# Layer two's pairs: the x tile and the last operand rounded at the end of the pair in front, and the next pair's transpositions ahead of the last output tile's addition

## The chip, the cores and the metric

The kernel runs on one core of a Trainium2 chip. A core has five engines that run their own queues of instructions side by side: TensorE (PE in the profile; its weight loads are listed apart as PEld), VectorE (DVE), ScalarE (ACT), GpSimd (POOL) and SyncE (SP), which here issues most of the DMAs. They wait for each other on semaphores. The metric is the time of one execution on the device in microseconds; with one core, the slowest core is the only one. All times below are microseconds.

## The reference

Four blocks act on one residual stream `x` of 2048 tokens by 512 features, in float32: linear attention, gMLP, and both once more with the same weights.

```python
# linear attention: 32 heads of 16
qkv = layernorm(x) @ wqkv                 # 512 x 1536
phi = lambda t: where(t > 0, t + 1, exp(t)) + 1e-6
kv  = einsum("bhsd,bhse->bhde", phi(k), v)
z   = einsum("bhsd->bhd", phi(k))
o   = einsum("bhqd,bhde->bhqe", phi(q), kv) / (phi(q) . z + 1e-6)
x   = x + o @ wo

# gMLP
t   = gelu(layernorm(x) @ w_in)           # 512 x 1792
z1, z2 = t[..., :896], layernorm(t[..., 896:])
g   = einsum("ts,bsf->btf", w_sp, z2) + b_sp
x   = x + (z1 * g) @ w_out
```

## The kernel before

The tokens are worked on in 16 tiles of 128. A *page* is a tile of 128 by 512 float32. TensorE multiplies in a rounded format, so every operand is kept as two parts: a *high* part, the value rounded (ACT, line 136, `high`), and a *low* part, the rounded rest (DVE, line 139, `low`). A product of two operands is then three matmuls (lines 150 to 152, `mm3`): high by high, high by low, low by high.

The change lies at the start of the second linear attention (`P1` with `L == 1`). Its input was normalised tile by tile while the first gMLP produced it, and went to DRAM (`norm`, line 394, on ACT; `send`). The first ten tiles are worked in five *pairs* `p` of tiles `a = 2p` and `b = 2p + 1`; the other six follow one by one in `second`. A pair does two things:

- The projections on K and Q. Two tiles together are brought through seven products (`P1`, `P7`, `P2`, `P6`, `P5`, `P4`, `P3`, in this order) in place of eight, six matmuls each, from sums of halves of the rows and sums of quarters of the weights (`joint`). The operands of a pair are `A` (tile a transposed), `B` (tile b, overwritten by a difference), `S` (a sum) and `D`, the *last operand*, half a page, that only `P3` reads.
- The accumulation of G, from which kv comes: `Gmm`, 24 matmuls of lines 150 to 152 in a pair, of the keys (phi of K) with the normalised tile itself, the *x tile*. These run one pair behind the projections: pair `p` makes the Gs of pair `p - 1`.

Around the products stand, by line:

- `rows` (448, DVE) turns a loaded tile by a transposition of 1.09; `first_part`, `second_part`, `sum_part` round A, B and S; `pair_sums` (841 to 846, DVE) makes the sums on half pages; `last_part` splits the half page D.
- ACT copies the accumulator of `P1` (bank `A`) into bank `B` (line 918), copies E to `w` (936) and B to `u` (949). DVE adds `X = w + B` (961 in pair 0, 977 in the others) and `c = E + u` (1008). `P2` and `P6` run behind the copy, `P3` behind X.
- phi: ACT does a relu and an exponential (871, 872, `pair_phi`), DVE the two halves of its sum (882, `pair_out`), four passes of ACT and four sets of halves a pair: A, X, c and B (`last`), the last two in the following pair. The keys are split into high (569, ACT) and low (905, DVE).
- The x tiles are loaded again from DRAM (`loadx`, 476, SP), and split by `x_high` (ACT) and `x_low` (DVE), lines 136 and 139.
- POOL adds up phi of K (`zsum`, 899). `wait_for` (892) is a tiny POOL operation that only orders a `zsum` behind a DVE operation.
- `own.staged()` are steps of background work for the last block, sums of quarters of `w_sp` (DMA in, DVE, POOL, DMA out). `side` holds pieces of the next weights `wo` and `win2`, whose rounding (136, 139, into `bg` tiles) stands in the last pair and in `second`.

The order on each engine is the order in which the program is written; nothing reorders it. Buffers are handed out by pools (`pages`, `banks`, `quads`): a DMA that loads a page waits until the reader of its last content is done. In pair 0 stands the end of the block in front too: `last_o`, which multiplies the last output tile of gMLP, adds it to the stream (2157, DVE), and computes its statistics (373, 375 on DVE, three small operations on POOL, the last at 384); then come `norm(15)` and `send(15)`.

```python
            if p:
                r = self.pair_phi(last)
                self.key_low(b - 2)
                self.x_high(b - 2)
                self.x_low(b - 2)
```

Of the kernel before, what the change touches and what calls it, by code (L numbers as in the profile page):

```python
# [15 lines left out]
P = 128  # L16
# [3 lines left out]
NT = S // P  # L20
# [7 lines left out]
PAIRS = (NT - DEFER) // 2  # L28
# [63 lines left out]
def mixer_kernel(ctx: ExitStack, tc: tile.TileContext, x_in, wqkv, wo_d, win1_d, win2_d, wsp_d, bsp_d, wout_d,  # L92
# [9 lines left out]
    pages = Slots(main, "pg", 23)  # L102
    quads = Slots(main, "qd", 6)
# [348 lines left out]
    class P1:  # L452
# [454 lines left out]
        def pair(self, p, side):  # L907
            a, b, own = 2 * p, 2 * p + 1, inner["N4"]
            nxt = p + 1 if p + 1 < PAIRS else None
            self.turn.load(a + 2)  # L910
            if nxt is not None:
                self.turn.load(b + 2)
            A = banks.get(PAGE)
# [5 lines left out]
            if p:  # L919
                c, last = self.open  # L920
                r = self.pair_phi(c)
                self.pair_out(c, r, b - 2, 0)
                self.K_high(b - 2)
            else:
                self.last_o()
                spare = quads.get([P, 2, 2, 512])
                own.home = Views(pages, spare)
                self.spare = spare
# [36 lines left out]
            if nxt is None:  # L965
                self.turn.row(a + 2)
            else:
                self.rows(a + 2)
                self.first_part(nxt)
                if p:  # L970
                    self.wait_for(self.ops[nxt, "A"][1][:, 0, 0:1])
            if p:
# [5 lines left out]
            r = self.pair_phi(X)  # L978
            if nxt is not None:
                self.rows(b + 2)  # L980
                self.pair_sums(nxt, 0)
                self.pair_sums(nxt, 1)
            else:
                self.T_high(a + 2)
# [8 lines left out]
            banks.put(X)  # L993
            if nxt is not None:
# [15 lines left out]
            self.product(B, "P3", p)  # L1010
            self.open = c, B
            if nxt is None:
                for _ in range(2):
                    side.popleft().piece()
            own.staged(False)
            if p >= PAIRS - 2:
                side[0].fetch()
                side[0].fetch()

        def second(self, side):  # L1020
            own = inner["N4"]
# [4 lines left out]
            for s in range(NT - DEFER + 1, NT + 2):  # L1026
                self.turn.load(s + 1)
                first = s == NT - DEFER + 1
                if first:
                    self.loadx(s - 1)  # L1030
                    self.loadx(s)
                self.loadx(s + 1)
                if first:
# [4 lines left out]
                    r = self.pair_phi(last)  # L1038
                    self.keys(s - 2)
# [723 lines left out]
    class P4:  # L1763
# [380 lines left out]
        def o(self, i, nxt):  # L2144
            q = self.zs.pop(i)
            b = banks.get(PAGE)
            for f in range(NF):
                mm3(b, (q[:, 0, f, :], q[:, 1, f, :]), self.wout[f], f == 0, f == NF - 1)
            quads.put(q)
            x = self.x.pop(i)  # L2150
            out = xs[2 * self.L + 2, i]
# [15 lines left out]
        def run(self, nxt):  # L2167
# [81 lines left out]
            for i in range(NT):  # L2249
# [6 lines left out]
                if nxt is not None and i == NT - 1:  # L2256
                    nxt.last_o = lambda: self.last(nxt)
                    break
                self.o(self.order[i], nxt)
                if nxt is not None:  # L2260
# [6 lines left out]
        def last(self, nxt):  # L2267
            i = NT - 1
            self.o(i, nxt)
            nxt.ms[i] = stats(nxt.x[i])  # L2270
            nxt.send(i - 1)
            self.join(i, nxt)

        def join(self, i, nxt):
# [34 lines left out]
            elif i > 11:  # L2309
                inner["N4"].staged()  # L2310
            if i == 15:
                for m in range(2):
                    for j in range(2):
                        w.parts(m, j, (4,))
                        w.done(m, j + 2)

# [46 lines left out]
```

## Time and profile before

| what | us |
|---|---|
| median of 3 runs (lowest to highest) | 1375.51 (1375.13 to 1376.03) |
| the profiled execution | 1374.01 |
| its span, first to last instruction | 1372.3 |
| PE busy in it | 1354.6 |
| DVE, ACT, POOL busy in it | 1061.7, 659.1, 504.6 |
| pair 0 and pair 1, from the first matmul of P1 on | 681.96, 697.17 |
| pairs 2, 3, 4 | 717.84, 735.62, 753.40 |
| behind the pairs; PE without a hole again | 771.10; 785.30 |

A row of a timeline has the start, the duration, the engine, the line, the operation, output and inputs (the program's names, buffer numbers left out), the shapes, and in brackets how long the engine sat idle before it and what ended that. A window is a stretch of time with the busy time and the number of instructions of each engine in it. The *granted clock* is the share of TensorE's full clock that it had in a stretch; 0.50 is half. PE's busy time counts a slow matmul at its slow length.

### The profile page before, as it was taken

The page shows a single profiled execution, that of the slowest core. Times are in us where ns is not written, and L with a number is a line of the kernel's source. Part 1 is how long each engine was busy: PE and PEld are TensorE (multiplying, and loading weights), DVE is VectorE, ACT ScalarE, POOL GpSimd, SP SyncE. Part 2 cuts the span into 40 slices and gives each one's busy share as a digit, 9 for nine tenths or more (in the row PEclk, how much of TensorE's full clock was granted, in tenths as well). Part 3 has the DMA queues.
Part 4 walks back from the last instruction along what each step waited for, and adds up shares of the span by engine and source line. Part 5 has one row for each costly group of instructions (what it writes and reads, how often), then busy time and mean ns, then how long its engine had stood idle before and what let it go on. Part 6 is the DMA issues. An engine that isn't in the chain of part 4 may idle for free.

```text
span 1372.3 us, 18447 instructions
## 1 busy us (share of the span) xinstructions
PE 1354.6 (99%) x6055; PEld 1126.8 (82%) x6055; DVE 1061.7 (77%) x1674; ACT 659.1 (48%) x1067; POOL 504.6 (37%) x603
## 2 busy tenths in 40 slices
PE   9999999999999999999989899999999999999998
PEld 7888888888888888888866688888888888888887
DVE  7885888876866888978977768877767798988642
ACT  7775543446443343424566665454456534534310
POOL 3333476533393347428411124633230011212240
PEclk9999999999999999999999999999999999999999
DMA  5762479966797988878652433766668798688552
GB/s 191 228 211 87 134 256 318 306 205 201 254 345 263 305 292 279 287 272 291 192 172 70 123 109 116 230 227 213 211 204 276 234 338 321 225 267 295 221 184 89
DMA packets 181744, 310.17 MB, mean 226 GB/s; under 512 B 15696, under 2 KB 67920, under 8 KB 177552
## 3 DMA queue, kind: packets, MB, share of 16 engines
q1 hardware_dynamic: 166544, 251.45, 56.2%
q0 software_dynamic: 11504, 51.12, 10.4%
q10 hardware_dynamic: 3600, 6.42, 1.3%
q8 instruction: 47, 0.77, 0.2%
q14 instruction: 49, 0.40, 0.1%
HBM read 211.68 MB, written 97.26 MB: 225 GB/s over the span
## 4 chain that ended last, share of the span: by engine, by line
PE 93%; DVE 4%; ACT 2%; issue 1%; DMA 0%; DVEq 0%; SPq 0%; ACTq 0%
PE bank L152 16%; PE bank L151 16%; PE bank L150 16%; PE bank L2019 9%; PE bank L2020 9%; PE bank L2021 9%; PE bank L1953 4%; PE bank L1952 4%; PE bank L1950 4%; PE bank L1389 1%; PE bank L1390 1%; PE bank L1388 1%; DVE pg L139 1%; DVE pg L448 1%; PE bank L404 1%
## 5 line engine op out<-in xcount | busy, mean ns | idle before, releaser
L2019 PE MATMUL bank<-qd,pg 128*128 128x512 f32 x544 | 211.7, 389 | 0.5 <-DVE bg L2078 0.5
L2021 PE MATMUL bank<-qd,pg 128*128 128x512 f32 x544 | 211.6, 389 | 0.0
L2020 PE MATMUL bank<-qd,pg 128*128 128x512 f32 x544 | 211.6, 389 | 0.0
L1866 DVE TENSOR_TENSOR qd<-qd,qd 128x1024 fp32r<-128x1024 f32 x104 | 139.4, 1341 | 63.0 <-ACT qd L1857 62.4
L1857 ACT ACTIVATE qd<-qd 128x1024 fp32r<-128x1024 f32 x104 | 110.1, 1058 | 121.2 <-DMA qd<-in_wsp_dram 42.6
L136 ACT ACTIVATE pg<-pg 128x512 fp32r<-128x512 f32 (+1 forms) x150 | 90.9, 613 | 115.0 <-DVE pg L448 37.2
L380 POOL TENSOR_SCALAR rs<-mv 128x1 f32<-128x1 f32 x96 | 44.7, 465 | 256.8 <-DVE mv L375 238.0
L2041 POOL TENSOR_TENSOR bg<-bg,pg 128x512 f32<-128x512 f32 x56 | 88.0, 1583 | 113.6 <-DMA pg<-z 100.9
L139 DVE TENSOR_TENSOR pg<-pg,pg 128x512 fp32r<-128x512 f32 (+1 forms) x147 | 108.4, 739 | 18.5 <-ACT pg L136 14.2
L2019 PEld LDWEIGHTS bank<-qd,pg 128*128 128x128 f32 x544 | 102.1, 188 | 22.1 <-issue 0.9
L2021 PEld LDWEIGHTS bank<-qd,pg 128*128 128x128 f32 x544 | 102.1, 188 | 21.2
L2020 PEld LDWEIGHTS bank<-qd,pg 128*128 128x128 f32 x544 | 102.1, 188 | 21.0
L152 PE MATMUL bank<-qd,pg 128*128 128x512 f32 x300 | 117.4, 391 | 0.0
L1609 POOL TENSOR_TENSOR pg<-pg,pg 128x512 f32<-128x512 f32 x50 | 78.5, 1570 | 104.8 <-DMA pg<-in_wsp_dram 80.0
L448 DVE STREAM_TRANSPOSE pg<-pg 128x512 f32<-128x512 f32 x79 | 86.3, 1092 | 10.5 <-DMA pg<-yt 6.2
L150 PE MATMUL bank<-bg,qd 128*128 128x448 f32 x256 | 94.0, 367 | 0.0
L151 PE MATMUL bank<-bg,qd 128*128 128x448 f32 x256 | 93.6, 366 | 0.0
L152 PE MATMUL bank<-bg,qd 128*128 128x448 f32 x256 | 93.4, 365 | 0.0
L1950 PE MATMUL bank<-qd,pg 128*128 128x512 f32 x224 | 87.1, 389 | 0.0
L1952 PE MATMUL bank<-qd,pg 128*128 128x512 f32 x224 | 87.1, 389 | 0.0
L1953 PE MATMUL bank<-qd,pg 128*128 128x512 f32 x224 | 87.1, 389 | 0.0
L150 PE MATMUL bank<-wo,qd 128*128 128x512 f32 x224 | 87.1, 389 | 0.0
(293 smaller groups left out, 3359.4 us busy)
## 6 DMA issues: line engine op xcount, KB each, us to landing
qd<-s SPq DMA_DIRECT2D x64, 512.0 KB, 4.5
qd<-n POOLq DMA_DIRECT2D x32, 1024.0 KB, 7.9
pg<-in_wsp_dram SPq DMA_DIRECT2D x99, 256.0 KB, 5.0
qd<-in_wsp_dram SPq DMA_DIRECT2D x40, 512.0 KB, 4.4
n<-pg SPq DMA_DIRECT2D x74, 256.0 KB, 4.7
pg<-z SPq DMA_DIRECT2D x56, 256.0 KB, 5.0
x<-pg SPq DMA_DIRECT2D x48, 256.0 KB, 2.7
pg<-x SPq DMA_DIRECT2D x48, 256.0 KB, 3.7
```

Of the source, the lines that this page charges most:

```text
L139: nc.vector.tensor_sub(l, src, h.bitcast(F32))
L150: nc.tensor.matmul(out, ah, bh, start=start, stop=False)
L151: nc.tensor.matmul(out, ah, bl, start=False, stop=False)
L152: nc.tensor.matmul(out, al, bh, start=False, stop=stop)
L1857: nc.scalar.activation(wh, r, AF.Copy)
L1866: nc.vector.tensor_sub(wl, r, wh.bitcast(F32))
L1950: m(out[i], h[:, o, f], w[:, o, 0], start=first and name in ("P1", "P2", "P5"), stop=False, skip_group_check=True)
L1952: m(out[i], h[:, o, f], w[:, o, 1], start=False, stop=False, skip_group_check=True)
L1953: m(out[i], l[:, o, f], w[:, o, 0], start=False, stop=last and name in ("P2", "P3", "P4"), skip_group_check=True)
L2019: m(out, h[:, o], w[:, 0, j, :], start=start, stop=False, skip_group_check=True)
L2020: m(out, h[:, o], w[:, 1, j, :], start=False, stop=False, skip_group_check=True)
L2021: m(out, l[:, o], w[:, 0, j, :], start=False, stop=stop, skip_group_check=True)
```

## The change

Seven moves, all in `pair`, `second` and what they call:

1. The x tile of `b` is split (`x_high`, `x_low`) at the end of the pair that loads it, behind `c`, and no longer in the following pair between phi and `w`.
2. The last operand of the next pair (`last_part`) is split there too; for pair 0 it keeps its place in pair 0, ahead of which `last_o` is gone.
3. In pair 0 the next pair's rows, first operand and half sums come ahead of the sum X. In pairs 1 to 3 only one of the two half sums (845, 846) moves, behind DVE's halves of X.
4. The last output tile's matmuls stay early (`o`); its addition, statistics, `norm(15)` and `send(15)` (`o_out`, `last`) come at the end of pair 0, behind the splits of points 1 and 2.
5. In the last pair, two of the four pieces of the next weight stand ahead of X, the other two ahead of `c`; their loads (`fetch`) move with them.
6. Behind the pairs, the x tile of the last `a` is split by `xsplit(s - 3)` ahead of G, and a `wait_for` and two `zsum` stand there.
7. Rows and x tiles are loaded at other places: those of pair 1 in front of pair 0, where `join` issues them during the block in front, and in `second` two of the three x tiles later. `join` no longer issues the quarter sums of the weights (`w.parts`), which pair 0 now does.

The core of the diff (line numbers behind it grow by up to 23):

```diff
@@ pair
             if p:
+                self.turn.load(a + 2)
...
                 self.K_high(b - 2)
-            else:
-                self.last_o()
...
-            self.last_part(p)
-            if p:
                 r = self.pair_phi(last)
                 self.key_low(b - 2)
-                self.x_high(b - 2)
-                self.x_low(b - 2)
+            else:
+                self.last_part(p)
+                w = self.joint
+                for m in range(2):
+                    for j in range(2):
+                        w.parts(m, j, (4,))
+                        w.done(m, j + 2)
+                o = self.before
+                o.ob = o.o(NT - 1, self)
+                self.send(NT - 2)
+                own.staged()
+                self.spare = quads.get([P, 2, 2, 512])
...
                 nc.scalar.activation(u, B, AF.Copy)
+                self.rows(a + 2)
+                self.first_part(nxt)
+                self.rows(b + 2)
+                self.pair_sums(nxt, 0)
+                self.pair_sums(nxt, 1)
                 self.product(A, "P2", p)
                 self.product(B, "P5", p)
                 X = banks.get(PAGE)
...
                 self.turn.row(a + 2)
-            else:
+                for _ in range(2):
+                    side.popleft().piece()
+                for _ in range(2):
+                    side[0].fetch()
+            elif p:
...
-            if p == 0:
-                self.norm(NT - 1)
-                self.send(NT - 1)
             self.loadx(b)
...
                 self.turn.load(b + 2)
-                for _ in range(2):
-                    side.popleft().piece()
-                side[0].fetch()
-                side[0].fetch()
+                side.popleft().piece()
+                side.popleft().piece()
...
             self.open = c, B
+            self.x_high(b)
+            if nxt is not None:
+                self.last_part(nxt)
+            self.x_low(b)
+            if p == 0:
+                self.last_o()
+                self.norm(NT - 1)
+                self.send(NT - 1)
+            own.staged(False)
@@ second
-                    self.xsplit(s - 2)
-                    self.keys(s - 3)
+                    self.K_high(s - 3)
+                    self.key_low(s - 3)
+                    self.xsplit(s - 3)
+                    self.wait_for(self.xhl[s - 3][1][:, 0:1])
+                    self.zsum(s - 2)
+                    self.zsum(s - 3)
                     self.Gmm(s - 5, (2, 3))
...
                     self.Gmm(s - 2)
-                    self.xsplit(s - 3)
+                    self.loadx(s)
+                    self.loadx(s + 1)
                     self.xsplit(s - 1)
```

**DVE, pair 0.** From the last output tile's addition (2157) to the sum X of pair 0 (961), before; the rows with `qd2` are quarter sums of the weights, `pg18_723` is the last operand's low part, 1750 a background step.

```order
L2157 TENSOR_TENSOR pg10_710_6858<-pg10_710_6858,bank3_182_6975 128x512
L373 BN_STATS st_6999<-pg10_710_6858 128x6
L375 BN_AGGR mv_7001<-st_6999 128x2
L139 TENSOR_TENSOR pg20_704_6803<-pg20_704_6803,pg19_717_6948 128x512
L1750 TENSOR_TENSOR pg2_718_6951<-pg2_718_6951,pg14_709_6856 128x512
L139 TENSOR_TENSOR qd2_159_7016<-pg15_665_6275,qd2_159_7016 128x256
L139 TENSOR_TENSOR qd2_159_7016<-pg6_677_6391,qd2_159_7016 128x256
L139 TENSOR_TENSOR qd2_159_7016<-pg16_666_6277,qd2_159_7016 128x4x2x32
L139 TENSOR_TENSOR qd2_159_7016<-pg9_678_6393,qd2_159_7016 128x4x2x32
L139 TENSOR_TENSOR pg18_723_7026<-pg5_698_6744,pg18_723_7026 128x256
L961 TENSOR_TENSOR bank1_183_7051<-w0_7029,bank7_181_6973 128x512
```

The same stretch of DVE now, from the first background step to X, which stands in line 973:

```order
L139 TENSOR_TENSOR pg20_704_6803<-pg20_704_6803,pg8_719_6952 128x512
L1770 TENSOR_TENSOR pg4_720_6955<-pg4_720_6955,pg14_709_6856 128x512
L448 STREAM_TRANSPOSE pg7_724_7028<-pg10_710_6858 128x4x128
L139 TENSOR_TENSOR pg5_725_7032<-pg7_724_7028,xA1_7030 128x512
L448 STREAM_TRANSPOSE pg15_726_7034<-pg0_716_6909 128x4x128
L841 TENSOR_TENSOR pg6_727_7036<-pg15_726_7034 128x256
L842 TENSOR_TENSOR pg15_726_7034<-pg7_724_7028,pg15_726_7034 128x256
L845 TENSOR_TENSOR pg6_727_7036<-pg6_727_7036,pg7_724_7028 128x256
L846 TENSOR_TENSOR pg7_724_7028<-pg7_724_7028,pg6_727_7036 128x256
L973 TENSOR_TENSOR bank1_183_7053<-w0_7018,bank7_181_6973 128x512
```

The two transpositions with their rounding and sums are ahead of X; the addition and the statistics of the last output tile are gone from here (five half pages stand in front of the first row shown).

**ACT, end of pair 0 and start of pair 1.** Before, with the normalisation (394) ahead of xB and xS, the operands B and S of pair 1, and then the copy (918):

```order
L394 ACTIVATE pg3_731_7080<-pg10_710_6858,nb_7006,rs_7003 128x4x4x32
L136 ACTIVATE xB1_7090<-pg9_729_7069 128x512
L136 ACTIVATE xS1_7094<-pg5_730_7071 128x512
L918 ACTIVATE bank4_186_7137<-bank2_184_7123 128x512
L871 ACTIVATE pg22_739_7139<-c0_7109 128x512
```

Now:

```order
L136 ACTIVATE xB1_7077<-pg15_726_7034 128x512
L136 ACTIVATE xS1_7081<-pg6_727_7036 128x512
L136 ACTIVATE pg2_738_7104<-pg3_733_7071 128x512
L136 ACTIVATE pg19_740_7107<-pg7_724_7028 128x256
L394 ACTIVATE pg15_741_7122<-pg1_711_6860,nb_7120,rs_7117 128x4x4x32
L922 ACTIVATE bank4_186_7146<-bank2_184_7132 128x512
L871 ACTIVATE pg6_744_7148<-c0_7096 128x512
```

The normalisation now stands directly ahead of the copy of pair 1, behind the x tile (`pg2_738`) and the last operand (`pg19_740`).

**ACT, pair 2.** From the rounding of S to `w` (936), before; `pg_767` is the last operand, `pg_769` the x tile.

```order
L136 ACTIVATE xS_7252<-pg_756_7231 128x512
L918 ACTIVATE bank_194_7290<-bank_192_7276 128x512
L871 ACTIVATE pg_764_7292<-c_7264 128x512
L872 ACTIVATE pg_764_7292<-pg_764_7292 128x512
L569 ACTIVATE pg_765_7297<-pg_758_7244 128x512
L136 ACTIVATE pg_767_7300<-pg_752_7209 128x256
L871 ACTIVATE pg_768_7303<-bank_186_7137 128x512
L872 ACTIVATE pg_768_7303<-pg_768_7303 128x512
L136 ACTIVATE pg_769_7307<-pg_757_7236 128x512
L936 ACTIVATE w_7311<-bank_193_7283 128x512
```

Now, with the copy in line 922 and `w` in 943:

```order
L136 ACTIVATE xS_7254<-pg_756_7231 128x512
L136 ACTIVATE pg_764_7274<-pg_759_7236 128x512
L136 ACTIVATE pg_766_7277<-pg_754_7211 128x256
L922 ACTIVATE bank_194_7299<-bank_192_7285 128x512
L871 ACTIVATE pg_769_7301<-c_7266 128x512
L872 ACTIVATE pg_769_7301<-pg_769_7301 128x512
L569 ACTIVATE pg_770_7306<-pg_760_7244 128x512
L871 ACTIVATE pg_772_7309<-bank_186_7146 128x512
L872 ACTIVATE pg_772_7309<-pg_772_7309 128x512
L943 ACTIVATE w_7313<-bank_193_7292 128x512
```

Both roundings moved from behind the copy to in front of it, so that nothing stands between the key's rounding, the phi of B, and `w`.

**DVE, the last pair.** From the x tile's low part to `c` (1008), before; `bg1_14` are the pieces of the next weight:

```order
L139 TENSOR_TENSOR pg5_827_7673<-pg16_811_7568,pg15_826_7672 128x512
L448 STREAM_TRANSPOSE pg17_828_7679<-pg3_814_7588 128x4x128
L977 TENSOR_TENSOR bank7_203_7688<-w4_7625,bank4_202_7604 128x512
L882 SCALAR_TENSOR_TENSOR pg2_831_7703<-bank7_203_7688,pg21_829_7690 128x256
L882 SCALAR_TENSOR_TENSOR z9_q1_7704<-bank7_203_7688,pg21_829_7690 128x256
L139 TENSOR_TENSOR pg0_832_7707<-pg17_828_7679,z10_h1_7693 128x512
L139 TENSOR_TENSOR bg1_14_7712<-pg8_812_7584,bg0_13_7711 128x512
L139 TENSOR_TENSOR bg1_14_7712<-pg13_813_7586,bg0_13_7711 128x512
L1008 TENSOR_TENSOR c4_7729<-bank6_201_7597,u4_7651 128x512
```

Now, with X in line 992 and `c` in 1019:

```order
L139 TENSOR_TENSOR pg11_829_7675<-pg12_813_7570,pg16_828_7674 128x512
L448 STREAM_TRANSPOSE pg22_830_7681<-pg2_817_7593 128x4x128
L139 TENSOR_TENSOR bg1_14_7684<-pg8_818_7595,bg0_13_7683 128x512
L139 TENSOR_TENSOR bg1_14_7684<-pg15_819_7597,bg0_13_7683 128x512
L992 TENSOR_TENSOR bank7_203_7700<-w4_7627,bank4_202_7613 128x512
L882 SCALAR_TENSOR_TENSOR pg5_835_7715<-bank7_203_7700,pg7_833_7702 128x256
L882 SCALAR_TENSOR_TENSOR z9_q1_7716<-bank7_203_7700,pg7_833_7702 128x256
L139 TENSOR_TENSOR pg21_836_7719<-pg22_830_7681,z10_h1_7705 128x512
L139 TENSOR_TENSOR bg1_14_7684<-pg6_831_7689,bg0_13_7683 128x512
L139 TENSOR_TENSOR bg1_14_7684<-pg19_832_7691,bg0_13_7683 128x512
L1019 TENSOR_TENSOR c4_7735<-bank6_201_7606,u4_7653 128x512
```

Two pieces now stand between the row and X, and two others between X and `c`, where two stood already.

More of the change, by code (lines that the diff above doesn't have):

```diff
@@ L909, in pair @@
             nxt = p + 1 if p + 1 < PAIRS else None
-            self.turn.load(a + 2)
-            if nxt is not None:
-                self.turn.load(b + 2)
+            if p:
+                self.turn.load(a + 2)
+                if nxt is not None:
+                    self.turn.load(b + 2)
+                else:
+                    side[0].fetch()
+                    side[0].fetch()
             A = banks.get(PAGE)
@@ L923, in pair @@
                 self.K_high(b - 2)
-            else:
-                self.last_o()
-                spare = quads.get([P, 2, 2, 512])
-                own.home = Views(pages, spare)
-                self.spare = spare
-            self.last_part(p)
-            if p:
                 r = self.pair_phi(last)
                 self.key_low(b - 2)
-                self.x_high(b - 2)
-                self.x_low(b - 2)
+            else:
+                self.last_part(p)
[9 more added lines that the diff above has]
+                self.spare = quads.get([P, 2, 2, 512])
             w = main.tile(PAGE, F32, tag=f"z{b + 2 if nxt is not None else 11}", bufs=1, name=f"w{p}")
@@ L978, in pair @@
             r = self.pair_phi(X)
[L979 removed]
+            if nxt is None:
+                self.T_high(a + 2)
+            elif p:
                 self.rows(b + 2)
                 self.pair_sums(nxt, 0)
[L982 to L984 removed]
             own.staged(False)
[L986 to L988 removed]
             self.loadx(b)
@@ L993, in pair @@
             banks.put(X)
+            if nxt is not None and p:
+                self.pair_sums(nxt, 1)
             if nxt is not None:
@@ L1011, in pair @@
             self.open = c, B
-            if nxt is None:
[L1013 to L1017, printed above, removed]
+            self.x_high(b)
+            if nxt is not None:
+                self.last_part(nxt)
[5 more added lines that the diff above has]
+            own.staged(False)
+            if p == 0:
+                own.home = Views(pages, self.spare)
+            if nxt is None:
                 side[0].fetch()
@@ L1028, in second @@
                 first = s == NT - DEFER + 1
[L1029 to L1032, printed above, removed]
+                self.loadx(s - 1 if first else s + 1)
                 if first:
@@ L2149, in o, with o_out @@
             quads.put(q)
+            return b
+        def o_out(self, i, nxt, b):
             x = self.x.pop(i)
@@ L2256, in run @@
                 if nxt is not None and i == NT - 1:
-                    nxt.last_o = lambda: self.last(nxt)
+                    nxt.before, nxt.last_o = self, lambda: self.last(nxt)
                     break
-                self.o(self.order[i], nxt)
+                self.o_out(self.order[i], nxt, self.o(self.order[i], nxt))
                 if nxt is not None:
@@ L2310, in join @@
                 inner["N4"].staged()
[L2311 to L2315, printed above, removed]
+            if i in (12, 13):
+                nxt.turn.load(i - 10)
     sums = Sums()
```

11 lines of the change are left out of this document (5 added, 6 removed).

## The prediction

> **What bounds the kernel now.** I read the page's first part, then windows cut at the first matmul of each pair, then the sum of PE's waits there, then the timelines of ACT, DVE and POOL.
>
> ```profile
> span 1372.3 us, 18447 instructions
> ...
> PE 1354.6 (99%) x6055; PEld 1126.8 (82%) x6055; DVE 1061.7 (77%) x1674; ACT 659.1 (48%) x1067; POOL 504.6 (37%) x603
> ```
>
> ```profile
> 697.17:717.84 20.67, 17.24 (x61) 11.97 (x61) 16.06 (x30) 12.87 (x23) 1.71 (x3) 0.92 0.51 166
> 717.84:735.62 17.78, 16.34 (x68) 11.92 (x67) 12.68 (x25) 10.58 (x19) 2.95 (x4) 1.00 0.21 59
> ...
> 771.10:785.30 14.20, 11.64 (x44) 8.91 (x42) 11.99 (x20) 9.69 (x18) 2.56 (x2) 0.88 0.41 126
> 785.30:812.50 27.20, 27.20 (x122) 22.52 (x120) 20.11 (x28) 16.64 (x29) 6.71 (x5) 1.00 0.51 150
> ...
> 699.99:703.40 3.41, 1.64 (x6) 1.07 (x7) 3.38 (x8) 1.46 (x3) 0.00 (x0) 1.00 0.78 238
> 703.40:706.81 3.41, 3.41 (x10) 2.64 (x9) 1.61 (x4) 2.00 (x4) 0.00 (x0) 0.50 0.97 325
> ...
> 778.49:781.90 3.41, 3.26 (x8) 2.58 (x9) 2.65 (x5) 1.64 (x4) 1.28 (x1) 0.50 0.00 0
> ```
>
> ```profile
> PE bank L150 <- ACT pg L136: 4.6, 5, 1.1
> ```
>
> Columns of a window: length, then busy time of PE, PEld, DVE, ACT, POOL, granted clock, DMA. PE has 99% of the whole, so only its holes can be won. From 785.30 it is dense again: 120 matmuls (five steps of 24) in 27.20, 0.2267 each. A pair has 42 matmuls of products and 24 for G, 66 x 0.2267 = 14.96; pair 2 takes 17.78, pair 1 takes 20.67, and the 42 matmuls behind the pairs (9.52) take 14.20. The longest sum of waits, 4.6 in five, is for ACT's rounding of the x tile, which the change moves. Two windows ran at clock 0.50.
>
> The pace is set by ACT and DVE, each feeding the other. My mark is ACT's copy L918, once a pair: 700.87 in pair 1, then 721.58, 739.37, 757.15; the end mark is PE at 785.30.
>
> **Term 1, the start of pair 1: +6.3.** In pair 0 DVE now makes the next pair's rows before the sum X, and the last output tile's addition comes at the end, followed by statistics, three POOL operations, ACT's normalisation, and only then the copy.
>
> ```profile
> 686.96 0.82 ACT L394 ACTIVATE pg<-pg,nb,rs 128x512 f32<-128x512 f32 x1 [0.57 <-POOL nb L384]
> 687.68 0.58 ACT L918 ACTIVATE bank<-bank 128x512 f32<-128x512 f32 x1
> 688.20 0.61 ACT L136 ACTIVATE pg<-pg 128x512 fp32r<-128x512 f32 x1
> 700.87 0.58 ACT L918 ACTIVATE bank<-bank 128x512 f32<-128x512 f32 x1
> ```
>
> ```profile
> 689.64 0.69 DVE L2157 TENSOR_TENSOR pg<-pg,bank 128x512 f32<-128x512 f32 x1 [3.51 <-PE bank L152]
> 691.25 0.66 DVE L139 TENSOR_TENSOR pg<-pg,pg 128x512 fp32r<-128x512 f32 x1
> 692.43 1.42 DVE L139 TENSOR_TENSOR qd<-pg,qd 128x256 fp32r<-128x256 f32 x4
> 694.11 0.69 DVE L961 TENSOR_TENSOR bank<-w,bank 128x512 f32<-128x512 f32 x1
> 695.38 1.08 DVE L448 STREAM_TRANSPOSE pg<-pg 128x512 f32<-128x512 f32 x1
> 697.76 1.11 DVE L448 STREAM_TRANSPOSE pg<-pg 128x512 f32<-128x512 f32 x1
> 700.50 0.69 DVE L139 TENSOR_TENSOR qd<-pg,pg 128x512 f32<-128x512 f32 x1
> ```
>
> ```profile
> 693.05 0.53 POOL L384 TENSOR_SCALAR nb<-mv,rs 128x1 f32<-128x1 f32 x1
> ```
>
> These are the timelines of ACT, DVE and POOL in pair 0. All before ACT's slot at 688.20 is the same in both. There now stands the rounding of half a page, the last operand of pair 0 (0.40 by a row of term 2), instead of the whole page's 0.61; its half residuals on DVE wait for it, so DVE goes on at 688.6. From start to start in the rows: five half pages 692.43 to 694.11 are 1.68; two steps of the background sums 691.25 to 692.43, 1.18; the first transposition with its rounding 695.38 to 697.76, 2.38; the second with four half sums 697.76 to 700.50, 2.74. X starts at 688.6 + 7.98 = 696.6 (694.11 before). P3 needs B free, and so X done, on PE: some 2 of idle time there, costed at nothing, because P2 of pair 1 waits for ACT's copy much later anyway; with the copy on time these 2 would be on the path. X, ACT's two passes of phi and DVE's two halves take 2.7 (0.69, 0.60, 0.63 and 0.66 with handoffs): 699.3. ACT's rounding of xB ends at 699.7; three roundings, c, the last operand, the x tile at 0.60 each and 0.34 for the half page: 703.0. The addition to the end of nb took 689.64 to 693.58, 3.94; there POOL ran beside two-input work of DVE, which now waits, so I take 3.5: 706.5. The normalisation holds ACT 0.72 (686.96 to the copy at 687.68 in that pair's start): the copy at 707.2, 6.3 late. Bounds: 707.7 with 3.94, 706.7 where handoffs are all shorter. P3 can start at 697.3, X's end, and P3, P1 and P7 are 18 matmuls, 4.1: PE is through at 701.4 and stands for some 6 before P2, which reads what the copy writes over.
>
> In that hole the clock is at stake. The row 699.99:703.40 has PE busy 1.64 of 3.41, and the window behind it ran at 0.50. Six matmuls of P2 and six of P6 at half pace end 5.1 behind the copy instead of 2.7; ACT gets to u, which needs them, 6.2 behind it (729.25 less 721.58 before, less the 1.45 below). So I cost the slow window at nothing here; the cover is 1.1. [...]
>
> **Term 2, three periods: -7.2.**
>
> ```profile
> 721.58 0.58 ACT L918 ACTIVATE bank<-bank 128x512 f32<-128x512 f32 x1 [2.17 <-PE bank L807]
> ...
> 724.39 0.40 ACT L136 ACTIVATE pg<-pg 128x256 fp32r<-128x256 f32 x1
> 724.70 0.58 ACT L871 ACTIVATE pg<-bank 128x512 f32<-128x512 f32 x1
> 725.31 0.63 ACT L872 ACTIVATE pg<-pg 128x512 f32<-128x512 f32 x1
> 725.85 0.61 ACT L136 ACTIVATE pg<-pg 128x512 fp32r<-128x512 f32 x1
> ...
> 727.56 0.63 ACT L569 ACTIVATE pg<-pg 128x512 fp32r<-128x512 f32 x1 [0.60 <-DVE pg L882]
> ...
> 729.25 0.58 ACT L949 ACTIVATE u<-bank 128x512 f32<-128x512 f32 x1
> ...
> 739.37 0.58 ACT L918 ACTIVATE bank<-bank 128x512 f32<-128x512 f32 x1 [2.17 <-PE bank L807]
> ```
>
> ```profile
> 757.15 0.58 ACT L918 ACTIVATE bank<-bank 128x512 f32<-128x512 f32 x1 [2.17 <-PE bank L807]
> ```
>
> The half page leaves: 724.39 to 724.70, 0.31. The exponential at 725.31 was followed by the x tile's rounding, w and a wait until 727.56, since DVE did the x tile's residual ahead of the halves; 2.25. Now the halves follow the exponential at once: 0.63, one half 0.42, two handoffs 0.06, so 1.11, which covers w. That is 1.14, with the half page 1.45. The same two roundings now stand at the pair's end, where ACT idles 2.17 before the copy (0.52 + 0.31 fit), and their residuals behind c on DVE, which then waits for ACT's passes. The period is 17.79 - 1.45 = 16.35, still above 14.96, so PE waits 1.4 a pair. Three periods are 49.0 against 757.15 - 700.87 = 56.3.
>
> **Terms 3 and 4, the last pair: -1.45 and +2.65.** The same 1.45 lies between copy and x tile there. But two pieces of the next weight now stand on DVE between the row and X.
>
> ```profile
> 766.06 0.69 DVE L139 TENSOR_TENSOR pg<-pg,pg 128x512 fp32r<-128x512 f32 x1 [0.30 <-issue]
> ...
> 772.18 0.68 DVE L1008 TENSOR_TENSOR c<-bank,u 128x512 f32<-128x512 f32 x1
> ...
> 777.21 1.37 DVE L139 TENSOR_TENSOR pg<-pg,pg 128x512 fp32r<-128x512 f32 x1
> ```
>
> ```profile
> 767.01 2.67 POOL L899 TENSOR_TENSOR pg<-pg,pg 128x512 f32<-128x512 f32 x2
> 776.76 1.28 POOL L578 TENSOR_TENSOR pg<-pg,pg 128x512 f32<-128x512 f32 x1 [7.09 <-DVE pg L574]
> ```
>
> Two residuals of 0.60 move X by 1.2, and c with it, as two still stand between X and c. They also fall beside POOL's two sums, 0.95 to 3.62 behind the x tile. The row at 777.21 has what that costs: 1.37 for 0.69, ended 0.54 behind POOL. If the engines take turns, the first residual ends 0.4 behind POOL's first sum, POOL's second follows, and the second residual ends behind that: 1.5 more. Bounds 0 and 2.0; I take 1.5, the only row being of a full wait. [...]
>
> **Term 5, behind the pairs: -3.2.**
>
> ```profile
> 775.30 0.61 ACT L569 ACTIVATE pg<-pg 128x512 fp32r<-128x512 f32 x1
> ```
>
> ```profile
> 776.48 0.51 PE L150 MATMUL bank<-pg,pg 128*128 128x512 f32 x1 [1.14 <-ACT pg L136]
> ...
> 778.64 0.80 PE L152 MATMUL bank<-pg,pg 128*128 128x512 f32 x1 [1.42 <-DVE pg L139]
> ```
>
> Before, c at 772.18 led to 785.30, 13.1. G waited for the x tile's high and then its residual (1.37), and a slow window followed. The x tile is now ready; G needs the keys alone: ACT's 775.30, 3.12 behind c, plus 0.66, then 0.4 for their residual, 24 matmuls 5.44, 0.3 to restart: 9.9. It is less 3.2, of which about 0.7 is the slow window.
>
> **The sum.** 6.3 - 7.2 - 1.45 + 2.65 - 3.2 = -2.9 on the profiled execution's 1374.01: 1371.1. The median of the runs is 1.5 above that execution; from 1375.51 the same gives 1372.6. The moved loads cost SP's queue a place and no time on an engine that waits: the rows' loads for pair 1 are issued two tiles sooner, and those of the pieces at the end keep their order.
>
> **Rivals.** Below 0.2% (2.75) a measurement of this kernel can hardly tell a change from none.
> - [...] Chance 0.15.
> - [...] Chance 0.30.
> - *Slower, the x tile comes late:*
>
> ```profile
> DMA to landing us min/median/max: 2.6/2.8/5.0
> ```
>
> These are the x tiles' loads, from SP's issue to landing. ACT now rounds the tile in the pair that loads it, ahead of the next copy, so lateness is paid in four pairs. The load is issued when DVE's halves of phi free a page. They go beside u, two of 0.42 from 729.25, and so ended 8.5 behind the copy at 721.58; now it is 1.45 sooner, 7.1. The rounding stands where ACT's 2.17 of idle time began, 14.2 behind the copy, so 7.1 is between them. It decides when four waits exceed the gain of 2.9 and 2.75 more, 1.4 each: landing after 8.5. The longest took 5.0. Chance 0.12, the part above the row for what else the moved issues meet on SP: 1379.
>
> The forecast has the rest, 0.43, with 1371.6 to 1373.2 of its own. The range, 1370.6 to 1374.8, holds it, the first rival, the second, and beyond these the 0.5 by which term 1 and term 4 are bounded on either side. Faster by over 0.2% (under 1372.76): 0.15 of the first rival and 0.33 of the forecast, 0.48; within: the forecast's other 0.10 and the second rival's 0.30, 0.40; slower: 0.12.
>
> **What would show it.** The copy of pair 1 near 707.2 and PE idle 6 before its P2; P3 of pair 0 waiting some 2; copies 16.35 apart; no PE wait of L150 on ACT L136 in pairs 2 to 4; two residuals of 1 us or more beside POOL in the last pair; one slow window near 707, none near 778. I am wrong if the copy is beyond 708, the period over 16.8, or the x tile's load ends ACT's idle time.

## The result, and the profile after

The changed kernel takes 1373.0 us in the median of 20 runs, the kernel before 1375.5 in the median of 20: a ratio of 0.9982 with a 95% interval of 0.9975 to 0.9989, or 2.5 less (1.5 to 3.4). The prediction was 1372.6, or 2.9 less. The profiled execution of the changed kernel took 1372.75.

The first part of the page after:

```profile
span 1370.9 us, 18450 instructions
...
PE 1352.4 (99%) x6055; PEld 1127.9 (82%) x6055; DVE 1067.0 (78%) x1674; ACT 658.5 (48%) x1067; POOL 505.7 (37%) x604
```

PE's waits of the changed kernel from 681.9 to 786: what it waited for, the total, how often, and the longest:

```profile
PE bank L805 <- ACT bank L922: 4.2, 1, 4.2
PE bank L805 <- DVE bank L973: 2.4, 1, 2.4
PE bank L805 <- DVE bank L992: 1.3, 1, 1.3
PE bank L807 <- DVE pg L139: 1.0, 2, 0.5
PE bank L150 <- ACT pg L569: 1.0, 1, 1.0
```

The old longest sum, 4.6 for the rounding of the x tile (L136), is gone. In its place PE waits once for the copy of pair 1 (L922), 4.2, once for the sum X of pair 0 (L973), 2.4, and once for X of the last pair (L992), 1.3.

ACT's timeline of the changed kernel at the five copies (L922), and the last row of the normalisation ahead of the second:

```profile
687.86 0.58 ACT L922 ACTIVATE bank<-bank 128x512 f32<-128x512 f32 x1
...
706.32 0.81 ACT L394 ACTIVATE pg<-pg,nb,rs 128x512 f32<-128x512 f32 x1 [5.16 <-POOL nb L384]
707.04 0.58 ACT L922 ACTIVATE bank<-bank 128x512 f32<-128x512 f32 x1
...
723.39 0.58 ACT L922 ACTIVATE bank<-bank 128x512 f32<-128x512 f32 x1 [0.86 <-PE bank L807]
...
756.12 0.58 ACT L922 ACTIVATE bank<-bank 128x512 f32<-128x512 f32 x1 [0.87 <-PE bank L807]
```

DVE's last pair, the same rows that the change moved: the two pieces ahead of X (L992), the two ahead of c (L1019), and c:

```profile
765.04 2.94 DVE L139 TENSOR_TENSOR bg<-pg,bg 128x512 fp32r<-128x512 f32 x2
767.91 0.68 DVE L992 TENSOR_TENSOR bank<-w,bank 128x512 f32<-128x512 f32 x1
...
771.24 1.29 DVE L139 TENSOR_TENSOR bg<-pg,bg 128x512 fp32r<-128x512 f32 x2
772.45 0.69 DVE L1019 TENSOR_TENSOR c<-bank,u 128x512 f32<-128x512 f32 x1
```

```profile
764.44 3.00 POOL L899 TENSOR_TENSOR pg<-pg,pg 128x512 f32<-128x512 f32 x2
```

The two residuals beside POOL's sums take 2.94, the two that stand alone 1.29.

To compare stages of two executions without what lies ahead of them, I measure from the copy of pair 0 on, and end behind the pairs at a row that both kernels have alike, the last pass of line 553 on ACT. Before:

```profile
847.99 0.58 ACT L553 ACTIVATE z_q<-bank 128x512 f32<-128x512 f32 x1
```

After:

```profile
845.25 0.58 ACT L553 ACTIVATE z_q<-bank 128x512 f32<-128x512 f32 x1
```

| stage, us | before | after | change | predicted |
|---|---|---|---|---|
| copy of pair 0 to copy of pair 1 (term 1) | 13.19 | 19.18 | +5.99 | +6.3 |
| to the copy of pair 4 (term 2) | 56.28 | 49.08 | -7.20 | -7.2 |
| to c of pair 4 (terms 3 and 4) | 15.03 | 16.33 | +1.30 | +1.2 |
| to the last pass of line 553 (term 5) | 75.81 | 72.80 | -3.01 | -3.2 |
| all | 160.31 | 157.39 | -2.92 | -2.9 |

The prediction's own end mark is PE without a hole again, behind the 42 matmuls that follow the pairs. Before, that was 785.30; after:

```profile
782.33 0.39 PE L150 MATMUL bank<-qd,z_h 128*128 128x512 f32 x1
```

By that mark term 5 is 9.88 behind c in place of 13.12, -3.24; 0.2 of it is gone again at the last pass of line 553.

### The profile page after: what moved, and what is told of

Same layout as the page of the kernel before. It is cut to its first block, busy times and chain, and to the rows that moved or that the text cites. A ratio compares the mean times of both kernels' runs of the same rounds, so it can differ in the third digit from the quotient of the medians.

```text
span 1370.9 us, 18450 instructions
## 1 busy us (share of the span) xinstructions
PE 1352.4 (99%) x6055; PEld 1127.9 (82%) x6055; DVE 1067.0 (78%) x1674; ACT 658.5 (48%) x1067; POOL 505.7 (37%) x604
## 4 chain that ended last, share of the span: by engine, by line
PE 92%; DVE 4%; ACT 3%; issue 1%; DMA 0%; POOL 0%; SPq 0%; DVEq 0%; ACTq 0%; POOLq 0%
PE bank L152 16%; PE bank L151 16%; PE bank L150 16%; PE bank L2039 9%; PE bank L2040 9%; PE bank L2041 9%; PE bank L1970 4%; PE bank L1973 4%; PE bank L1972 4%; PE bank L1409 1%; PE bank L1410 1%; PE bank L1408 1%; DVE pg L448 1%; PE bank L404 1%; PE bank L1149 1%
## 5 line engine op out<-in xcount | busy, mean ns | idle before, releaser
L136 ACT ACTIVATE pg<-pg 128x512 fp32r<-128x512 f32 (+1 forms) x151 | 91.3, 613 | 119.1 <-DVE pg L448 35.0
L2061 POOL TENSOR_TENSOR bg<-bg,pg 128x512 f32<-128x512 f32 x56 | 91.4, 1642 | 111.9 <-DMA pg<-z 104.9
L150 PE MATMUL bank<-bg,qd 128*128 128x448 f32 x256 | 94.0, 367 | 0.0
L150 PE MATMUL bank<-wo,qd 128*128 128x512 f32 x224 | 87.1, 389 | 0.0
```

What stands on the lines that cost most here:

```text
L150: nc.tensor.matmul(out, ah, bh, start=start, stop=False)
```

## The experiments

Each kernel was timed in five rounds or more beside the kernel before on the same chip; its median is told against that. In the table, "stage" is the length from the copy of pair 0 to the last pass of line 553, less the 157.4 of the changed kernel. It comes from one profiled execution and is the sharper measure, since the runs of one kernel lie 1.2 to 4.1 apart, while the length of term 1, 19.18 in the changed kernel, came out as 19.18, 19.19 and 19.22 in the three kernels that leave it alone (e2, e3, e8). The last column is the median's difference to before, less the changed kernel's -2.5.

| kernel | median | before | ratio (95%) | stage | by the medians |
|---|---|---|---|---|---|
| e1, normalisation later | 1369.06 | 1375.94 | 0.9948 (0.9935 to 0.9960) | -4.1 | -4.4 |
| e2, pieces back | 1370.77 | 1375.94 | 0.9960 (0.9946 to 0.9974) | -2.8 | -2.7 |
| e3, no sums | 1371.89 | 1375.94 | 0.9968 (0.9956 to 0.9981) | -1.7 | -1.6 |
| e5, hole filled | 1373.66 | 1375.94 | 0.9983 (0.9974 to 0.9991) | 0.0 | +0.2 |
| e4, before with rounding alone | 1369.83 | 1375.16 | 0.9960 (0.9946 to 0.9974) | -3.6 | -2.8 |
| e7, all of it | 1364.98 | 1375.16 | 0.9927 (0.9914 to 0.9939) | -8.4 | -7.7 |
| e8, tail undone | 1374.43 | 1375.16 | 0.9996 (0.9987 to 1.0005) | +2.4 | +1.8 |
| e9, X first | 1375.76 | 1375.16 | 1.0000 (0.9991 to 1.0008) | +1.7 | +3.1 |

**Term 1, the start of pair 1.** The first question was whether the normalisation is what holds the copy of pair 1.

```diff
             if p == 0:
                 self.last_o()
+            if p == 1:
                 self.norm(NT - 1)
                 self.send(NT - 1)
```

> The changed kernel, with only the normalisation and the storing of the last output tile moved from the end of pair 0 to the end of pair 1; its addition and statistics stay. Theory (term 1 is ACT's wait for the statistics, 5.16 in the changed kernel, with the 0.72 of the normalisation behind it): the copy of pair 1 starts as soon as P1 is through, near 702 in place of 707.04; DVE's halves of c then wait for the addition and the statistics, which end at 704.9, so about 0.7 comes back; 4.3 sooner than the changed kernel, 6.8 sooner than before. Rival (pair 1 is bound by PE at half clock and by DVE, and ACT's wait only fills time that is lost anyway): 1 sooner or less, with PE waiting for DVE in pair 1.

ACT and DVE in this kernel:

```profile
700.11 0.92 ACT L136 ACTIVATE pg<-pg 128x512 fp32r<-128x512 f32 x2
702.06 0.58 ACT L922 ACTIVATE bank<-bank 128x512 f32<-128x512 f32 x1 [1.03 <-PE bank L807]
...
705.10 0.63 ACT L569 ACTIVATE pg<-pg 128x512 fp32r<-128x512 f32 x1 [1.26 <-DVE pg L882]
```

```profile
704.58 0.18 DVE L375 BATCH_NORM_AGGREGATE mv<-st 128x2 f32<-128x6 f32 x1
704.67 0.39 DVE L882 SCALAR_TENSOR_TENSOR pg<-c,pg 128x256 f32<-128x256 f32 x1
```

The copy stands at 702.06 and waits only for the end of P1 on PE (1.03). The halves of c (L882) follow the statistics without a gap, and ACT waits 1.26 for them where it waits 0.49 elsewhere: the 0.7 that comes back. 5.0 less 0.7 is the measured 4.1 to 4.4. The rival is out.

The other half of term 1, X behind the transpositions, was undone by itself:

```diff
                 nc.scalar.activation(u, B, AF.Copy)
-                self.rows(a + 2)
-                self.first_part(nxt)
-                self.rows(b + 2)
-                self.pair_sums(nxt, 0)
-                self.pair_sums(nxt, 1)
                 self.product(A, "P2", p)
                 self.product(B, "P5", p)
                 X = banks.get(PAGE)
                 nc.vector.tensor_add(X, w, B)
                 r = self.pair_phi(A)
+                self.rows(a + 2)
+                self.first_part(nxt)
+                self.rows(b + 2)
+                self.pair_sums(nxt, 0)
+                self.pair_sums(nxt, 1)
```

> The changed kernel, with the sum X of pair 0 ahead of both transpositions of the next pair's rows, as before. Theory (DVE has no idle time from there to the copy of pair 1, and X ahead of the rows only makes them wait for P5): P5 ends later than DVE would need it, DVE idles, and the copy of pair 1 comes 2.0 later, near 709; the time 2.0 more. Rival (PE's wait of 2.4 for X is the price of the new order, and goes): 0 to 2 less.

DVE in this kernel:

```profile
692.36 0.69 DVE L1770 TENSOR_TENSOR pg<-pg,pg 128x512 f32<-128x512 f32 x1
695.20 0.69 DVE L968 TENSOR_TENSOR bank<-w,bank 128x512 f32<-128x512 f32 x1 [2.15 <-PE bank L807]
```

DVE now idles 2.15 for P5, and most of that stays: the copy of pair 1 came 20.92 behind that of pair 0 in place of 19.18, and the stage is 1.7 longer. PE's wait for X is gone here, and nothing is won by it. So the wait of 2.4 in the changed kernel is no loss to be undone: the order that brings it saves 1.7. With this half undone the whole gain is gone in the runs (1.0000 to before); their 3.1 more is above the stage's 1.7, within the intervals of the two ratios.

**The clock in pair 1.** Windows of the changed kernel, cut where the clock changed; the columns are those of the prediction:

```profile
694.19:697.60 3.41, 1.05 (x6) 0.55 (x4) 3.31 (x7) 0.48 (x2) 0.00 (x0) 1.00 0.41 138
697.60:701.01 3.41, 3.41 (x8) 2.68 (x9) 3.06 (x7) 3.38 (x7) 0.00 (x0) 0.51 0.36 118
...
704.39:707.80 3.41, 0.13 (x1) 0.13 (x2) 0.40 (x2) 1.48 (x3) 1.05 (x3) 1.00 0.21 79
707.80:711.21 3.41, 3.41 (x9) 2.66 (x10) 1.53 (x4) 2.85 (x6) 0.00 (x0) 0.51 0.90 278
```

Two slow windows, where one was predicted: the first follows PE's wait for X. To see what the second costs, PE was given work in its hole.

```diff
             self.product(E, "P7", p, True)
+            if p == 1:
+                for _ in range(3):
+                    self.product(E, "P7", p, True)
             B = banks.get(PAGE)
```

> The changed kernel, with P7 of pair 1 done three times more (18 matmuls, 4.1, whose result is the same), so that PE works through the hole of 4.2 ahead of P2 of pair 1. Theory (the slow window behind the hole is covered, since ACT needs P6 only at u): P2 and P6 run at full clock, and the time is the same within 0.3. Rival (the slow window is on the path): 1.3 to 1.7 sooner.

PE in this kernel, around the start of P2:

```profile
707.59 0.39 PE L807 MATMUL bank<-bg,pg 128*128 128x512 f32 x1
709.66 0.50 PE L805 MATMUL bank<-qd,xA 128*128 128x512 f32 x1 [1.69 <-ACT bank L925]
710.00 0.40 PE L806 MATMUL bank<-qd,xA 128*128 128x512 f32 x1
```

P2 ran at full pace (0.63 each in the changed kernel, 0.40 here), the clock was 1.00 throughout, and the stage is the same (157.41 and 157.39). The slow window was covered, as the prediction costed it. This kernel also had the wait for X (2.32) and no slow window behind it, so neither of the two slow windows cost the changed kernel anything. The second came behind 3.41 in which PE was busy 0.13, the first behind 3.41 in which it was busy 1.05.

Six of the ten profiled kernels have this wait for X, 2.3 to 2.4, and four of them a slow window behind it; the two without are those with the hole filled and with the tail undone (e8, below). Read in slices of 0.2, the slow stretches start at 703.40 and 778.49 in the kernel before, 22 lengths of 3.413 apart, and at 697.65 and 707.89 in the changed kernel, three apart. There the wait for X (695.18 to 697.54) lies between two such edges, 694.24 and 697.65. With the tail undone a slow stretch starts at 777.93; counted back from it in steps of 3.413, an edge at 696.01 cuts the wait (695.03 to 697.40). That leaves PE 2.43 and 2.02 of work in the two windows, and the clock stayed full: PE was through P7 sooner and waited 5.8 for the copy of pair 1, where it waits 4.2 in the changed kernel. Laid out as windows of 3.413 from the edges, the executions before and after say the same from 10 us after their start to their end: a window at full clock with PE busy 1.64 or less was followed by half the clock, one with 1.81 or more was not. Behind each of the four slow windows named here, with PE busy 3.26 to 3.41, the clock was full again. So 1.81 of 3.413 was enough work in these two executions to keep the clock, and 1.64 was not. In the kernel with the hole filled no slow stretch shows where the windows lie.

**Term 4, the last pair.** First the pieces of the next weight were put back, and then, with the pieces where the change puts them, POOL's sums were left out.

```diff
-                for _ in range(2):
-                    side.popleft().piece()
-                for _ in range(2):
-                    side[0].fetch()
...
-                side.popleft().piece()
-                side.popleft().piece()
+                for _ in range(2):
+                    side.popleft().piece()
+                for _ in range(2):
+                    side[0].fetch()
...
             if nxt is None:
+                for _ in range(2):
+                    side.popleft().piece()
                 side[0].fetch()
```

> The changed kernel, with the four pieces of the next weight in the last pair back at their old places (two behind X, two behind P3). Theory (term 4: two residuals of 0.6 and a wait of 1.5 for POOL): c of the last pair 14.2 behind the copy in place of 16.33 to 16.4, and 2.7 sooner in all. Rival one (no wait for POOL): 1.2 sooner. Rival two (the pieces only change places, and what is saved ahead of c is lost behind it): 0, with PE waiting 2 to 3 more behind the pairs.

ACT and DVE in this kernel, the last copy and c:

```profile
756.74 0.58 ACT L922 ACTIVATE bank<-bank 128x512 f32<-128x512 f32 x1 [0.87 <-PE bank L807]
```

```profile
770.22 0.69 DVE L1017 TENSOR_TENSOR c<-bank,u 128x512 f32<-128x512 f32 x1
```

From the last copy to c: 756.74 to 770.22, 13.48, where the changed kernel has 16.33. (The expected 14.2 was worked out wrongly: 16.33 less 2.7 is 13.6.) The stage is 2.8 shorter, so rival one, 1.2, is out, and with no longer wait behind the pairs rival two as well.

```diff
-                self.wait_for(self.xhl[a - 2][1][:, 0:1])
-                self.zsum(b - 2)
+                if nxt is not None:
+                    self.wait_for(self.xhl[a - 2][1][:, 0:1])
+                    self.zsum(b - 2)
+                else:
+                    pages.put(self.r.pop(b - 2))
...
-            if p:
+            if p and nxt is not None:
                 self.zsum(a - 2)
+            elif p:
+                pages.put(self.r.pop(a - 2))
```

> The changed kernel, leaving out of the computation POOL's two additions of phi of K in the last pair. Theory (the two residuals there wait for POOL): their 2.94 becomes 1.3, as the other two of the pair take, and the time 1.6 less. Rival (the second residual waits for ACT's rounding of its piece, or for the load): 2.9 again, and the time the same.

DVE in this kernel, the row that was 2.94:

```profile
765.02 1.26 DVE L139 TENSOR_TENSOR bg<-pg,bg 128x512 fp32r<-128x512 f32 x2
766.20 0.69 DVE L997 TENSOR_TENSOR bank<-w,bank 128x512 f32<-128x512 f32 x1
```

2.94 became 1.26 with nothing else changed ahead of it, and the stage 1.7 shorter. So DVE's two residuals took 1.68 more beside POOL's additions than without them; the prediction's lower bound for this wait, 0, is out.

**Terms 2, 3 and 5, the rounding.** The rounding alone, in the kernel before:

```diff
             else:
                 self.last_o()
...
-            self.last_part(p)
+                self.last_part(p)
             if p:
                 r = self.pair_phi(last)
                 self.key_low(b - 2)
-                self.x_high(b - 2)
-                self.x_low(b - 2)
...
             self.open = c, B
+            self.x_high(b)
+            if nxt is not None:
+                self.last_part(nxt)
+            self.x_low(b)
...
-                    self.xsplit(s - 2)
                     self.keys(s - 3)
```

> The kernel before, with only the splitting of the x tile and of the next pair's last operand moved to the pair's end; pair 0, the last pair's pieces and the loads stay. Theory: terms 2 and 3 without terms 1 and 4, but the x tile of pair 0 comes late there, because its load is queued on SP behind the storing of the last output tile, which waited for the normalisation until 699.51: issued at 700.3, landed at 703.1, rounded, then the copy of pair 1 near 704.1 in place of 700.87; after that periods of 16.3 and 13.5 from the last copy to c, and a little less behind the pairs: 6 sooner than before, so 3.5 sooner than the changed kernel. Rival (the tile is there in time): the copy near 701.7, and 8.5 sooner than before.

ACT in this kernel:

```profile
700.38 0.62 ACT L136 ACTIVATE xS<-pg 128x512 fp32r<-128x512 f32 x1
703.49 0.94 ACT L136 ACTIVATE pg<-pg 128x512 fp32r<-128x512 f32 x2 [2.50 <-DMA pg<-xt]
704.34 0.58 ACT L918 ACTIVATE bank<-bank 128x512 f32<-128x512 f32 x1
```

SP's queue in the same stretch:

```profile
699.55 0.37 SPq L428 DMA_DIRECT2D xt<-pg  x1
700.33 0.37 SPq L476 DMA_DIRECT2D pg<-xt  x1
```

The load of the x tile (L476) stands on SP behind the storing of the normalised last tile (L428), is issued at 700.33, and ACT waits 2.50 for it. The copy is at 704.34, as expected; the periods behind it are 16.36, and c of the last pair comes 13.46 behind the last copy. In the changed kernel the storing comes later and the load goes out at 692.49:

```profile
692.49 0.37 SPq L476 DMA_DIRECT2D pg<-xt  x1
```

The stage is 6.6 shorter than before, and the median 5.3. So the prediction's slow rival, a late x tile, is a real mechanism, and what keeps it away in pair 0 is that the change moves `send(15)` behind this load.

The tail was undone in the changed kernel, for the last pair's x tile alone:

```diff
-            self.x_high(b)
             if nxt is not None:
+                self.x_high(b)
                 self.last_part(nxt)
-            self.x_low(b)
+                self.x_low(b)
...
+                    self.xsplit(s - 2)
                     self.K_high(s - 3)
                     self.key_low(s - 3)
```

> The changed kernel, with the x tile of the last pair split behind the pairs again, as before, ahead of the keys of the other tile. Theory (term 5: 3.2, of which 0.7 the slow window): 1.0 later if no slow window follows, 2.6 if one does; PE waits for the x tile ahead of G. Rival (the tile's split stood there beside other waits): the same time.

PE in this kernel, and then its windows behind the pairs:

```profile
776.68 0.50 PE L150 MATMUL bank<-pg,pg 128*128 128x512 f32 x1 [1.46 <-ACT pg L136]
778.15 0.79 PE L152 MATMUL bank<-pg,pg 128*128 128x512 f32 x1 [0.73 <-DVE pg L139]
```

```profile
775.00:778.40 3.40, 1.21 (x4) 0.62 (x4) 2.50 (x6) 2.78 (x5) 0.00 (x0) 0.93 0.00 0
778.40:781.80 3.40, 3.40 (x10) 2.63 (x11) 2.70 (x4) 1.43 (x3) 2.33 (x3) 0.57 0.33 101
```

The waits for the x tile's two halves are back, and in this execution the slow window with them: 2.4 more by the stage, 1.8 by the medians. The two waits are 2.19 together, 1.0 more than the waits for the keys in the changed kernel (0.95 and 0.22); the rest of the 2.4 goes to the slow window.

**A version that beats both.** The gains were put together: the roundings stay, the parts that cost are undone or spread.

```diff
             if p == 0:
                 self.last_o()
+            if p == 1:
+                self.ms[NT - 1] = stats(self.x[NT - 1])
+            if p == 2:
                 self.norm(NT - 1)
                 self.send(NT - 1)
```

Beside this stand the pieces as in e2, `last` without its statistics, and in pair 0 the sum X behind the first of the two transpositions.

> The changed kernel, with: the last output tile's addition kept at the end of pair 0, its statistics at the end of pair 1, its normalisation and storing at the end of pair 2; the four pieces of the next weight at their old places; in pair 0 the sum X between the next pair's two transpositions, as in the other pairs. Theory: the two undone parts add up (4.4 and 2.7, as measured apart), and DVE's statistics no longer stand ahead of the halves of c (1.0), X 0.3: 8.4 sooner than the changed kernel, 10.9 sooner than before. Rival (what stands behind the pairs has its own pace, or the gains overlap): 6 sooner than the changed kernel or less, with new waits of PE behind 780.

1364.98 against 1375.16: 10.2 less than before. Against the changed kernel that is 7.7 less by the medians and 8.4 by the stage, where 8.4 was expected. ACT in this kernel:

```profile
698.60 0.61 ACT L136 ACTIVATE pg<-pg 128x512 fp32r<-128x512 f32 x1
700.33 0.42 ACT L136 ACTIVATE pg<-pg 128x256 fp32r<-128x256 f32 x1 [1.11 <-DVE z_q L882]
700.65 0.58 ACT L922 ACTIVATE bank<-bank 128x512 f32<-128x512 f32 x1
702.67 0.64 ACT L871 ACTIVATE pg<-c 128x512 f32<-128x512 f32 x1 [1.44 <-DVE c L1017]
```

The copy of pair 1 comes 11.97 behind that of pair 0 (13.19 before, 19.18 after); behind it the pace is again DVE's, on which ACT waits for c.

## Why the prediction was right

Each term held within about 0.3, as the table of stages shows, and the reasons held under the runs that took them away one by one.

- **Term 1.** The place was right (the copy at 707.04, forecast 707.2), and the mechanism was shown by the first experiment. Two of its steps were off and nearly cancelled, which is luck: the last tile's addition started at 703.20, not 703.0, and from there to the end of nb passed 3.1, not 3.5, since POOL's three operations, with DVE idle beside them, took 0.22, 0.57 and 0.26 where they had taken 0.50, 0.86 and 0.53. The forecast hole of PE, "some 6", was 4.16, because P3 and the first two matmuls of P1 ran in a slow window that the prediction had not foreseen, and P7 ended at 703.5, not at 701.4; the time was the copy's, so nothing came of it.
- **The clock behind the hole** was covered, as costed; filling the hole gave nothing (0.0). The upper end of the range, 1374.8, allows for 1.7 lost to it; no run shows such a loss: the stage is 157.41 with the hole filled and 157.39 without.
- **Term 2.** 49.08 for the three periods, against 49.0. The period is 16.35 to 16.4, the wait of L150 for ACT's L136 is gone from every pair.
- **Terms 3 and 4.** 1.30 against 1.2. Whether the residuals wait beside POOL's sums was the choice between 1.2 and 2.65 here, and the wait was shown: 1.7 goes when POOL's sums go (1.5 was forecast), 2.8 when the pieces go.
- **Term 5.** 3.01 against 3.2 at line 553, 3.24 at the prediction's own end mark. That the x tile's lateness stood on the path was shown. The slow window's share was put too low at 0.7: before, eight steps of PE from 778.64 on took 3.45, and at full pace they take about 1.9 (my estimate: one first step of 0.34, as at 709.66 with the hole filled, and seven of 0.2267, the pace from 785.30 on). As the term was taken from end to end, the sum did not suffer; the price of a run before without this window did.
- **The loads.** "A place and no time" was true of the sum, but the sentence missed a gain: without the move of `send(15)` the x tile's load would have come late in pair 0, and the copy of pair 1 with it. The kernel with the rounding alone (e4) showed it. This was the slow rival, which got its chance for the later pairs, where it did not occur.

One thing stays open: for the profiled execution the prediction had 1371.1, and it took 1372.75. The two profiled executions differ by only 1.26 (1374.01 and 1372.75), less than the medians' 2.5 and the stage's 2.92, though these two lie within the interval. The one before lay 1.5 below its median, the one after 0.25. At the last pass of line 553 they differ by 2.74, and still by 2.79 at a DVE row in the last block. DVE's timeline there, before:

```profile
1217.94 0.69 DVE L1750 TENSOR_TENSOR pg<-pg,pg 128x512 f32<-128x512 f32 x1 [1.96 <-DMA pg<-in_wsp_dram]
1218.55 0.55 DVE L1893 TENSOR_TENSOR z_z<-z_z,z_z 128x384 f32<-128x384 f32 x1
```

After, with POOL's row below it:

```profile
1215.15 0.69 DVE L1770 TENSOR_TENSOR pg<-pg,pg 128x512 f32<-128x512 f32 x1 [1.94 <-DMA pg<-in_wsp_dram]
1215.77 1.68 DVE L1913 TENSOR_TENSOR z_z<-z_z,z_z 128x384 f32<-128x384 f32 x1
```

```profile
1215.74 1.29 POOL L2061 TENSOR_TENSOR bg<-bg,pg 128x512 f32<-128x512 f32 x1 [5.36 <-DMA pg<-z]
```

PE's wait there, before and then after:

```profile
PE bank L2019 <- DVE bg L2078: 0.5, 1, 0.5
```

```profile
PE bank L2039 <- DVE bg L2098: 1.6, 1, 1.6
```

So, 430 behind the change, the same DVE operation fell beside a POOL addition and took 1.1 more, and PE waited 1.6 in place of 0.5: 1.1 was given back in that execution. Where the remaining 0.4 went is not traced. How many executions of either kernel have it, the medians can't tell; of the ten profiled kernels seven had the long wait (1.4 to 1.7) and three the short (0.4 to 0.5).

## What to carry to other kernels

Where two engines feed each other, mark one operation that comes once a round and read the change as lengths between marks: four lengths told here what 2.5 of 1375 could not. Work that is moved "out of the way" is paid where it lands if an engine must pass it in order: the last tile's normalisation had no hurry, and cost 4 as the last thing ahead of a copy and next to nothing one pair later. And before a rounding is pulled forward, look at what the load that it needs is queued behind.

## What was not expected of the hardware

- The same hole of PE of 2.3 to 2.4, the wait for X, was followed by a stretch at half the clock where it lay within one window of 3.41 (PE busy 1.05 of it in the changed kernel) and by none where a window's edge cut it (2.43 and 2.02 busy, with the tail undone). One execution has such a stretch, the next has not.
- One DVE operation, hundreds of microseconds behind any changed line, took 1.68 beside a POOL addition in the changed kernel and 0.55 in the kernel before, and PE's wait there was 1.6 in place of 0.5. That wait came and went from kernel to kernel: 1.4 to 1.7 in seven, 0.4 to 0.5 in three.
